# Threshold attention and a GELU MLP: scores of two query slots in one visit, three PSUM banks per head

## The chip, the cores and the metric

The kernel runs on one core of a Trainium2 chip. The metric is the device time of one execution in microseconds; the median of several runs is compared. The engines are named as in the profile: PE (TensorE matmul), PEld (its weight loads), DVE (VectorE), ACT (ScalarE), POOL (GpSimd) and SP (SyncE, which here only issues DMAs).

## The reference

Attention over 8 batches, 8 heads, 576 positions, head dimension 64, with a threshold in place of a plain softmax, and then two matmuls with an exact GELU between them. All is float32.

```
scores = q @ k.T / sqrt(64)
keep   = scores >= max(scores, -1) - tau          # others count as -1e9
attn   = exp(scores - max) of the kept; attn /= sum + 1e-9
x      = (attn @ v), laid out as (8*576, 8*64) = (4608, 512)
out    = gelu(x @ w_in) @ w_out                   # w_in 512x2048, w_out 2048x512
```

## The kernel before

The 64 heads are taken as 32 pairs, two heads of 64 rows on the 128 partitions. Four pairs belong to one batch. The first four pairs ("early") are worked through in another manner while the weights arrive and are converted; the change starts just behind them, and the 28 later pairs are what matters here.

A late pair has five slots: four of 128 queries (i = 0 to 3) and one, i = NC = 4, with the last 64 queries of both heads. For one slot, the kernel issues

1. `scores` (L394): PE forms q times k, 128 queries by 576 keys, for head e = 0 and e = 1. The two heads use the upper and the lower 64 rows of the array at the same time. Each head has a tile `sc` of two PSUM banks with 288 columns in each; there are two such tiles (`bufs=2`), four banks. Slot NC needs one tile only, with all 128 rows.
2. `softmax_head` (L406): for each head a maximum on DVE (L415, `nmx`), a threshold on POOL (L416, `thr`), the exp on ACT (L418), which writes the tile `p` in SBUF.
3. `softmax_tail` (L421): for each head one DVE pass (L434) that compares the scores with the threshold, multiplies the exps by the outcome and sums the row. It is the last reader of `sc`.
4. `turn_p` (L488): DVE transposes `p` in blocks of 32 into `turned_p`. `regroup` (L504) then lets SP issue the DMAs that bring it into `pT`, the layout that the next matmul needs: eight for slots 0 and 1, eight for slots 2 and 3, four for NC.

When a pair is through, `divisors` (L466) turns and spreads the row sums. In the next pair, at slot WEIGH = 2, `weigh_v` (L522) multiplies `pT` by v in two calls of 320 and 256 columns, each into a PSUM tile `xT`, and ACT copies it to `xall` (L547), the input of the MLP. There is one `pT` for each head, so the DMAs of a pair wait until the weighing of the pair before is done. `divide` (L556) multiplies by the divisors on POOL. `scale_q` and `turn_qk` prepare q and k of the next pair on ACT and DVE.

The MLP is issued in small steps between the slots. `block_steps` (L602) is a generator over one block of 256 tokens: a tile `hT` takes eight matmuls (L613) of 256 columns, four for each of two groups of 128 features; `gelus` (L573) puts its GELU on ACT, with up to `lag` tiles left waiting; then `o_ps` (L628) takes 2 x 16 matmuls of 512 columns. `fill` (L637) draws steps as long as a debt of PE time lasts. The debt of a slot comes from a goal for the number of blocks done by that slot (`GOAL`) times a share by slot:

```
    PARTS = 1.3, 1.3, 0.2, 1.3, 0.9
```

GELU and exp use different tables on ACT; `table` (L596) loads the one for exp again, ahead of the next exps, if a GELU ran since. `hT`, `o_ps`, `xT` and a few early tiles share four PSUM banks (tag "mm"), so all eight banks are in use. The order on each engine is the program's order: the kernel is written under a manual schedule.

The last ten blocks of the MLP come after all attention, as a recursive (Strassen-like) product (`last_blocks`, L973); it uses the same two tags of banks.

Of the kernel before, what the change touches and what calls it, by code (L numbers as in the profile page):

```python
# [18 lines left out]
def kernel(  # L19
# [28 lines left out]
    nc = tc.nc  # L48
# [30 lines left out]
    dram = ctx.enter_context(tc.tile_pool(name="dram", bufs=1, space=bass.MemoryType.DRAM))  # L79
    ps = ctx.enter_context(tc.tile_pool(name="ps", bufs=4, space=PSUM))  # L80

# [62 lines left out]
    nc.vector.memset(zeros, 0.0)  # L144
    idle = ps.tile([P, 2 * P], FP32, tag="mm", name="idle")
    for _ in range(3):
# [154 lines left out]
    def turn_qk_early(p):  # L301
# [12 lines left out]
        for name in "qk":  # L314
            t = s[name]
            tr = ps.tile([P, NC, P], FP32, tag="mm", name="tr")
            for c in range(NC):
                for e in range(2):
                    nc.tensor.matmul(tr[e * D:(e + 1) * D, c, :], lhsT=t[:, e, c, :], rhs=ident, start=True, stop=True)
            src = tr.rearrange("p c s -> p (c s)")  # L320
            if name == "q":
                nc.scalar.activation(qT, src, AF.Copy, bias=0.0, scale=q_scale)
            else:
                copy(kT[:, TAIL:S], src)
        tr = ps.tile([P, NC, P], FP32, tag="mm", name="tr")
        for j, name in enumerate("qk"):
# [12 lines left out]
    def turn_p_early(p, i):  # L339
# [11 lines left out]
        for e in range(n):  # L351
            tr = ps.tile([P, NC, P], FP32, tag="mm", name="tr")
            for c in range(NC):
                turn(tr[:, c, :], e * (S + TAIL) + c * P)
            if i < NC:
                nc.scalar.copy(s["pT"][e][:, 0:NC, i * P:(i + 1) * P], tr)  # L356
# [4 lines left out]
        tails = s["pT"][0][:, NC, :]  # L361
        tr = ps.tile([P, NC, P], FP32, tag="mm", name="tr")
        turn(tr[:, 0, :], MAIN if i < NC else S - P)
# [29 lines left out]

    def scores(p, i):  # L394
        s = st[p]
        n = 1 if i == NC else 2
        sc = s["sc", i] = [ps.tile([P, 2, 512], FP32, tag="sc", name="sc", bufs=2) for _ in range(n)]
        for h in range(2):
            for e in range(n):
                rows = slice(0, P) if i == NC else slice(e * D, (e + 1) * D)  # L400
                lhsT = s["q_tail"] if i == NC else s["qT"][rows, i * P:(i + 1) * P]
                at = h * HALF + (TAIL if p < EARLY and e == 0 else 0)
                nc.tensor.matmul(  # L403
                    sc[e][:, h, 0:HALF], lhsT=lhsT, rhs=s["kT"][rows, at:at + HALF], start=True, stop=True)

    def softmax_head(p, i):  # L406
# [6 lines left out]
        for e in range(n):  # L413
            sc = s["sc", i][e][:, :, 0:HALF]
            nc.vector.tensor_reduce(nmx[:, e:e + 1], sc, axis=AXIS.XY, op=ALU.max, negate=True)  # L415
            nc.gpsimd.tensor_scalar(  # L416
                thr[:, e:e + 1], nmx[:, e:e + 1], -1.0, tau_eff, op0=ALU.mult, op1=ALU.subtract)
            nc.scalar.activation(  # L418
                w[:, e * S:(e + 1) * S].rearrange("p (h s) -> p h s", h=2), sc, AF.Exp, bias=nmx[:, e:e + 1], scale=1.0)

    def softmax_tail(p, i):  # L421
# [10 lines left out]
        for e in range(n):  # L432
            row = w[:, e * S:(e + 1) * S].rearrange("p (h s) -> p h s", h=2)
            nc.vector.scalar_tensor_tensor(  # L434
                row, sc[e][:, :, 0:HALF], thr[:, e:e + 1], row, op0=ALU.is_ge, op1=ALU.mult, accum_out=den[e])
        if p < EARLY:
# [8 lines left out]
    def divide_early(p, lo, hi):  # L445
# [3 lines left out]
        b, hp = divmod(p, HP)  # L449
        tr = ps.tile([P, 512], FP32, tag="mm", name="tr")  # L450
        for i in range(lo // P, -(-hi // P)):
# [69 lines left out]

    def weigh_v(p, lo, hi):  # L522


        b, hp = divmod(p, HP)
        s = st[p]
        xT = ps.tile([P, 512], FP32, tag="mm", name="xT")
        for c in range(KR):
            for e in range(2):
                f = slice(e * D, (e + 1) * D)  # L530
                to = xT[f, 0:hi - lo]
                if p < EARLY:
                    rhs = s["pT"][0 if c == NC else e][:, c, lo:hi]
                else:
                    to = to.rearrange("p (g s) -> p g s", s=2 * Q)
                    rhs = by_64(s["pT"][e])[:, lo // (2 * Q):hi // (2 * Q), c, :]
                nc.tensor.matmul(  # L537
                    to, lhsT=s["v"][:, e, c, :], rhs=rhs, start=(c == 0), stop=(c == KR - 1))
        for n, o, at, size in in_blocks(b, lo, hi):
            if n not in x_blk:  # L540
# [61 lines left out]
    def block_steps(n):  # L602
# [3 lines left out]
        for j in range(N_DF):  # L606
            if j % 2 == 0:
                hT = None
            for c in range(N_DM):
                yield NS_IN, (j * P // PIECE + 1) * N_DM  # L610
                if hT is None:
                    hT = ps.tile([P, 2, TOK], FP32, tag="mm", name="hT")
                nc.tensor.matmul(hT[:, j % 2, :], lhsT=w_in_sb[c][:, j * P:(j + 1) * P], rhs=x_blk[n][:, c, :],  # L613
                                 start=(c == 0), stop=(c == N_DM - 1))
            if j % 2:
                late.append((g, j, hT))
                gelus(lag[0])
        x_free.append(x_at.pop(n))
        for m in range(TOK // P):
            for j in range(N_DF):  # L620
# [5 lines left out]
                if j == 0:  # L626
                    o = ps.tile([P, 512], FP32, tag="mm", name="o_ps")
                nc.tensor.matmul(o[:, 0:d_model], lhsT=g[j][:, m * P:(m + 1) * P], rhs=w_out_sb[j],  # L628
                                 start=(j == 0), stop=(j == N_DF - 1))
            o_sb = op.tile([P, d_model], FP32, tag="o_sb", name="o_sb")  # L630
            nc.scalar.copy(o_sb, o[:, 0:d_model])
            row = n * TOK + m * P
            nc.sync.dma_start(out[row:row + P, :], o_sb)

    mlp = {"n": 0, "steps": None, "next": None, "debt": 0.0, "layer": 0}

    def fill(ns, tokens):  # L637

        mlp["debt"] += ns
        while True:  # L640
# [7 lines left out]
            took, need = mlp["next"]  # L648
            if mlp["debt"] <= 0 or need > converted[0]:
                break  # L650
# [153 lines left out]
    def bank(tag, n):  # L804
        if tag == "sc":
            return ps.tile([P, 2, 512], FP32, tag="sc", name="bank", bufs=2)[:, 0, 0:n]
        return ps.tile([P, 512], FP32, tag="mm", name="bank")[:, 0:n]

# [221 lines left out]

    parts = [(range(2), HP), (range(2, SLOTS), HP)] + [(range(SLOTS), 1)] * (NP - HP)
    slots = []
# [19 lines left out]

    PARTS = 1.3, 1.3, 0.2, 1.3, 0.9

# [5 lines left out]
    for n in range(len(slots) + WEIGH + 1):  # L1060
        p, i = slots[n] if n < len(slots) else divmod(n, SLOTS)
        early = p < EARLY
        last = slots[n - 1] if 0 < n <= len(slots) else None
        if p < NP:
            scores(p, i)
            softmax_head(p, i)
            add_low_bits()
# [4 lines left out]
        elif n == len(slots):  # L1072
            early_end.close()
            weights_first()
        gelus(0)
        if n == BATCH:
            gelus_held()
        table()
        for args in due:
            weigh_v(*args)  # L1080
            divide_early(*args)
        due = []
        if p > EARLY and i == WEIGH:
            for lo, hi in (0, WIDE), (WIDE, S):
                weigh_v(p - 1, lo, hi)
            if p == NP:
                divide(p - 1)
        owed += (goal(n) - goal(n - 1)) * BLK_NS * (PARTS[i] if not early and p < NP else 1.0)
        if early:
# [7 lines left out]
        if p < NP:  # L1097
            softmax_tail(p, i)
        if p < NP and not early:
            turn_p(p, i)  # L1100
        if p < NP and not early:
            if i == 2:
                regroup(p, 1)
            if i > 2:
                regroup(p, i)
            if i == NC:
                divisors(p)
# [10 lines left out]
        if n == BATCH:  # L1118
            for t in pd_tail + [turned_p[:, e, h, :, :] for e in range(2) for h in range(2)]:
                nc.gpsimd.memset(t[:, NB:4 * KR, :], 0.0)  # L1120
        if EARLY < p < NP and i == DIVIDE:
            divide(p - 1)
        if p >= HP and i == 1 and p + 2 < NP:
            loads = load_steps(p + 2)
        if p >= HP:
            next(loads, None)
        if p >= HP and i == 1 and p + 1 < NP or p == HP - 1 and i == 2:
            scale_q(p + 1)
        if p >= HP - 1 and i == 2 and p + 1 < NP:
            turn_qk(p + 1)  # L1130
        convert(0 if n == 0 else 1200 if n < 3 else 2200 if n < BATCH - 1 else 1e9)
        if not early:
            lag[0] = 2 if p < NP else 0
            if n != BATCH:
                fill(owed, tokens)
                owed = 0.0
# [7 lines left out]
        elif n == BATCH + 1:  # L1144
            tokens = S
        elif p > EARLY and i == DIVIDE and p % HP == 0 or p == NP and i == WEIGH:
            tokens = p // HP * S
            leaving += [n for n in AWAY if n in x_blk and (n + 1) * TOK <= tokens]
        elif leaving and i < 2:
            put_away(leaving.pop(0))  # L1150
    fill(1e12, B * S)
    late_end.close()
    last_blocks()

# [31 lines left out]
```

## Time and profile before

| what | value |
|---|---|
| median of 3 runs | 1352.92 us (1352.58 to 1353.92) |
| the profiled execution, its own time | 1353.51 us |
| its span, first to last instruction | 1351.4 us |
| late pairs, from the first weighing in their manner to the 27th | 184.7 to 848.1 us |
| end of the last weighing | 882.6 us |
| granted clock of TensorE | 0.993 over the span, 1.00 in the late pairs |

In the profile, a line as "L418 ACT ACTIVATE p<-sc,nmx" is a group of instructions of one source line, with the tile written before the arrow and those read behind it. Busy time is the time in which an engine had an instruction under way; a matmul's end is modelled, so consecutive matmuls overlap in the records and the distance between their starts is what they cost PE. A float32 matmul is two records. "128*128", "64*128" and "128*64" name the part of the array that a matmul uses, rows by columns. In the timeline, the first number is the start, the second the length of a run of equal instructions, and what stands in brackets is idle time of the engine before it and who ended it.

### The profile page before, as it was taken

How to read it: one execution, taken by the hardware profiler on the slowest of the kernel's cores; microseconds unless marked ns; L12 is line 12 of the kernel's file. 1: busy time of each engine (PE TensorE's matmuls, PEld its weight loads, DVE VectorE, ACT ScalarE, POOL GpSimd, SP SyncE). 2: the span in 40 equal slices, each digit the busy share in tenths (PEclk: the TensorE clock that was granted, in tenths of full speed). 3: DMA queues.
4: the chain of work that ended last, by engine and by line, in shares of the span. 5: the costliest groups of instructions: out<-in, count | busy, mean ns of one | idle time of the engine just before them, and what ended most of it. 6: DMA issues, size and time to landing. Idle time of an engine off the chain costs nothing.

```text
span 1351.4 us, 19821 instructions
## 1 busy us (share of the span) xinstructions
PE 1323.0 (98%) x6282; PEld 893.8 (66%) x6282; DVE 1048.1 (78%) x1997; ACT 605.0 (45%) x1027; POOL 659.0 (49%) x1097
## 2 busy tenths in 40 slices
PE   8799899999999999999999999999999999999998
PEld 6476557467467557557557557568787787877877
DVE  6987677788888888888888888874758698385765
ACT  7876527548547538537638636413201112211120
POOL 5785354555555554554554551144363513635530
PEclk9899999999999999999999999999999999999999
DMA  8642276677777787687687777500000041000003
GB/s 268 187 151 52 58 164 156 146 162 185 155 180 182 161 193 178 160 207 172 153 208 180 155 179 152 117 9 0 1 0 1 14 112 32 0 1 0 1 0 78
DMA packets 209781, 152.39 MB, mean 113 GB/s; under 512 B 113360, under 2 KB 193088, under 8 KB 209680
## 3 DMA queue, kind: packets, MB, share of 16 engines
q1 hardware_dynamic: 188224, 112.53, 37.5%
q0 software_dynamic: 21024, 38.32, 9.9%
q8 instruction: 51, 0.84, 0.3%
q14 instruction: 50, 0.41, 0.1%
q10 hardware_dynamic: 432, 0.30, 0.1%
HBM read 55.97 MB, written 12.52 MB: 51 GB/s over the span
## 4 chain that ended last, share of the span: by engine, by line
PE 93%; DVE 3%; ACT 3%; DMA 1%; issue 1%; SPq 0%; POOL 0%; DVEq 0%; ACTq 0%; POOLq 0%
PE bank L801 34%; PE o_ps L628 17%; PE hT L613 16%; PE sc L403 14%; PE xT L537 11%; ACT p L418 1%; DMA x<-xall 1%; DVE nmx L415 1%; DVE p L434 1%; PE tr L349 1%; ACT pT L356 1%; DVE power L212 0%; ACT power L202 0%; DVE power L210 0%; PE tr L456 0%
## 5 line engine op out<-in xcount | busy, mean ns | idle before, releaser
L418 ACT ACTIVATE p<-sc,nmx 128x576 f32<-128x576 f32 x288 | 201.9, 738 | 284.0 <-DVE nmx L415 283.7
L434 DVE SCALAR_TENSOR_TENSOR p<-sc,thr,p 128x576 f32<-128x576 f32 x288 | 225.3, 816 | 70.1 <-ACT p L418 68.6
L416 POOL TENSOR_SCALAR thr<-nmx,tau_eff 128x1 f32<-128x1 f32 x288 | 88.0, 307 | 368.0 <-DVE nmx L415 355.8
L415 DVE TENSOR_REDUCE nmx<-sc 128x1 f32<-128x576 f32 x288 | 205.4, 750 | 53.5 <-PE sc L403 52.3
L613 PE MATMUL hT<-xall,w_in 128*128 128x256 f32 x1024 | 241.8, 385 | 0.0
L628 PE MATMUL o_ps<-w_out,g 128*128 128x512 f32 x512 | 236.8, 603 | 0.0
L613 PEld LDWEIGHTS hT<-xall,w_in 128*128 128x128 f32 x1024 | 189.4, 190 | 50.0 <-issue 23.0
L683 DVE TENSOR_TENSOR c<-c,bank 128x320 f32<-128x320 f32 x304 | 147.3, 488 | 33.6 <-PE bank L801 20.1
L683 DVE TENSOR_TENSOR o<-o,bank 128x256 f32<-128x256 f32 x240 | 99.8, 420 | 93.7 <-PE bank L801 88.7
L403 PE MATMUL sc<-kT,qT 64*128 64x288 f32 x960 | 161.8, 431 | 9.3 <-DVE p L434 8.6
L537 PE MATMUL xT<-pT,v 128*64 128x256 f32 (+1 forms) x1280 | 169.3, 418 | 0.8 <-DVE pT L360 0.5
L628 PEld LDWEIGHTS o_ps<-w_out,g 128*128 128x128 f32 x512 | 93.1, 190 | 109.1 <-issue 106.8
L498 DVE STREAM_TRANSPOSE turned_p<-p 128x1152 f32<-128x1152 f32 x112 | 154.4, 1378 | 3.9
L403 PEld LDWEIGHTS sc<-kT,qT 64*128 64x128 f32 x960 | 92.4, 187 | 83.8 <-issue 69.7
L537 PEld LDWEIGHTS xT<-pT,v 128*64 128x64 f32 x1280 | 93.0, 140 | 75.4 <-issue 15.1
L801 PE MATMUL bank<-w_out,c 128*128 128x256 f32 x480 | 120.2, 381 | 0.5 <-DVE o L683 0.5
L269 POOL DMA_DIRECT2D v<-in_v_dram x208 | 110.9, 536 | 3.9 <-issue 1.9
L801 PEld LDWEIGHTS bank<-w_out,c 128*128 128x128 f32 x480 | 89.9, 190 | 18.8 <-DVE o L683 3.0
L854 ACT ACTIVATE c<-c 128x320 f32<-128x320 f32 (+1 forms) x80 | 46.9, 623 | 114.6 <-DVE c L683 114.6
L683 POOL TENSOR_TENSOR c<-c,g 128x320 f32<-128x320 f32 (+1 forms) x40 | 50.5, 1271 | 67.4 <-DVE c L683 67.4
L801 PE MATMUL bank<-t_out,c 128*128 128x256 f32 x320 | 82.7, 381 | 0.0
L801 PE MATMUL bank<-t_out,g 128*128 128x256 f32 x320 | 82.1, 379 | 0.0
(179 smaller groups left out, 1775.1 us busy)
## 6 DMA issues: line engine op xcount, KB each, us to landing
pT<-turned_p SPq DMA_DIRECT2D x448, 160.0 KB, 3.6
pT<-pd_tail SPq DMA_DIRECT2D x112, 80.0 KB, 3.0
q<-in_q_dram POOLq DMA_DIRECT2D x104, 72.0 KB, 3.4
k<-in_k_dram POOLq DMA_DIRECT2D x104, 72.0 KB, 3.2
inv<-turned SPq DMA_DIRECT2D x54, 128.0 KB, 3.9
v<-in_v_dram POOLq DMA_DIRECT2D x156, 40.0 KB, 3.1
out_dram<-o SPq DMA_DIRECT2D x40, 128.0 KB, 2.4
xall<-in_moe_w_out_dram POOLq DMA_DIRECT2D x9, 512.0 KB, 3.8
```

Source lines behind the costliest of these rows:

```text
L269: eng.dma_start(t[r:P:4, e, 0:n, :], rows[:, r * KR:r * KR + n, :])
L403: nc.tensor.matmul(sc[e][:, h, 0:HALF], lhsT=lhsT, rhs=s["kT"][rows, at:at + HALF], start=True, stop=True)
L415: nc.vector.tensor_reduce(nmx[:, e:e + 1], sc, axis=AXIS.XY, op=ALU.max, negate=True)
L416: nc.gpsimd.tensor_scalar(thr[:, e:e + 1], nmx[:, e:e + 1], -1.0, tau_eff, op0=ALU.mult, op1=ALU.subtract)
L418: nc.scalar.activation(w[:, e * S:(e + 1) * S].rearrange("p (h s) -> p h s", h=2), sc, AF.Exp, bias=nmx[:, e:e + 1], scale=1.0)
L434: nc.vector.scalar_tensor_tensor(row, sc[e][:, :, 0:HALF], thr[:, e:e + 1], row, op0=ALU.is_ge, op1=ALU.mult, accum_out=den[e])
L498: nc.vector.transpose(turned_p[:, :, i // 2, 0:NB, i % 2 * Q:(i % 2 + 1) * Q], w.rearrange("p (e b i) -> p e b i", e=2, i=Q))
L537: nc.tensor.matmul(to, lhsT=s["v"][:, e, c, :], rhs=rhs, start=(c == 0), stop=(c == KR - 1))
L613: nc.tensor.matmul(hT[:, j % 2, :], lhsT=w_in_sb[c][:, j * P:(j + 1) * P], rhs=x_blk[n][:, c, :], start=(c == 0), stop=(c == N_DM - 1))
L628: nc.tensor.matmul(o[:, 0:d_model], lhsT=g[j][:, m * P:(m + 1) * P], rhs=w_out_sb[j], start=(j == 0), stop=(j == N_DF - 1))
L683: eng.tensor_tensor(out, a, b, op=ALU.add)
L801: nc.tensor.matmul(to, lhsT=l, rhs=r, start=start and k == 0, stop=k == len(pairs) - 1, skip_group_check=not start)
```

## The change

From slot n = JOIN = BATCH + 2 = 22 on, the third slot of the first late pair:

- The scores of slots 0 and 1, and those of 2 and 3, are formed in one visit of PE ("joint"): 12 matmuls of 192 columns in place of twice four of 288. A head's tile has now three banks; slot i takes columns 0 to 191 of each, slot i+1 columns 192 to 383. Two such tiles take six banks; the tag "mm" keeps two. The pools are closed and opened anew at JOIN, and once more before `last_blocks` (four and 2 x 2 banks again).
- The slots of a pair come in the order 0, 1, NC, 2, 3. `pos` is the place in a pair. The heads and tails of the softmax of both slots are issued one after the other: four maxima and exps, then four masked passes, then a transpose (the second one in the next place).
- `weigh_v` takes both spans in one call, and its two outputs lie in one tile of the tag "sc" in place of two tiles of "mm". The copies to `xall` come after all its matmuls.
- `regroup` of slots 0, 1 and of NC comes at place 2, that of slots 2 and 3 at place 4, right before `divisors`. `divide`, the loads of q, k and v, `scale_q` and `turn_qk` keep their places, which now belong to other slots.
- GELUs are issued right behind their tile (`lag` 0 in place of 2), and once layer one is under way `fill` goes on until the open `hT` tile is complete (`close`). The shares by place are 1.1, 1.1, 0.6, 1.1, 1.1.

```diff
-    ps = ctx.enter_context(tc.tile_pool(name="ps", bufs=4, space=PSUM))
+    def lay_out_banks(name, mm, width):
+        banks.close()
+        space["pool"] = banks.enter_context(tc.tile_pool(name=name, bufs=mm, space=PSUM, reuse_waits="tile"))
+        space["width"] = width
+    def score_banks(name):
+        return space["pool"].tile([P, space["width"], 512], FP32, tag="sc", name=name, bufs=2)
+    lay_out_banks("ps", 4, 2)
...
-    def scores(p, i):
+    def scores(p, i, both=False):
...
+        units = [i, i + 1] if both else [i]
+        wide = S // 3 if both else HALF
+        sc = [score_banks("sc") for _ in range(n)]
+        for k, c in enumerate(units):
+            s["sc", c] = [t[:, 0:S // wide, k * wide:(k + 1) * wide] for t in sc]
+            for h in range(S // wide):
+                for e in range(n):
...
+                    nc.tensor.matmul(
+                        s["sc", c][e][:, h, :], lhsT=lhsT, rhs=s["kT"][rows, at:at + wide], start=True, stop=True)
...
-    def fill(ns, tokens):
+    def fill(ns, tokens, close=False):
...
-            if mlp["debt"] <= 0 or need > converted[0]:
+            if not (close and mlp["open"]) and mlp["debt"] <= 0 or need > converted[0]:
                 break
...
-    parts = [(range(2), HP), (range(2, SLOTS), HP)] + [(range(SLOTS), 1)] * (NP - HP)
+    parts = [(range(2), HP), (range(2, SLOTS), HP)] + [((0, 1, NC, 2, 3), 1)] * (NP - HP)
...
-    PARTS = 1.3, 1.3, 0.2, 1.3, 0.9
+    PARTS = 1.1, 1.1, 0.6, 1.1, 1.1
+    JOIN = BATCH + 2
...
+        pos = n % SLOTS
+        if n == JOIN:
+            gelus(0)
+            lay_out_banks("ps_joined", 2, 3)
+        single = n < JOIN or i == NC
+        if n > JOIN and (single or i % 2 == 0):
+            table()
         if p < NP:
-            scores(p, i)
-            softmax_head(p, i)
+            if single:
+                scores(p, i)
+                softmax_head(p, i)
+            elif i % 2 == 0:
+                scores(p, i, both=True)
+                softmax_head(p, i)
+                softmax_head(p, i + 1)
...
-        if p > EARLY and i == WEIGH:
-            for lo, hi in (0, WIDE), (WIDE, S):
-                weigh_v(p - 1, lo, hi)
+        if p > EARLY and pos == WEIGH:
+            xT = score_banks("xT")
+            weigh_v(p - 1, [(0, WIDE), (WIDE, S)], [xT[:, half, :] for half in range(2)])
...
-            softmax_tail(p, i)
+            if single:
+                softmax_tail(p, i)
+            elif i % 2 == 0:
+                softmax_tail(p, i)
+                softmax_tail(p, i + 1)
         if p < NP and not early:
             turn_p(p, i)
-        if p < NP and not early:
-            if i == 2:
+            if pos == 2:
                 regroup(p, 1)
-            if i > 2:
-                regroup(p, i)
-            if i == NC:
+                regroup(p, NC)
+            if pos == 4:
+                regroup(p, 3)
                 divisors(p)
...
-            lag[0] = 2 if p < NP else 0
+            lag[0] = 2 if n < JOIN - 1 else 0
             if n != BATCH:
-                fill(owed, tokens)
+                fill(owed, tokens, n == JOIN - 1 or n >= JOIN and mlp["layer"] == 1)
...
     late_end.close()
+    lay_out_banks("ps_last", 4, 2)
     last_blocks()
```

## The prediction

> **What bounds the kernel now.** I read the busy shares first, then the table by stretches for the 26 pairs of heads between the first and the 27th weighing after the early part (184.7 to 848.1 us), then the timeline of one pair.
>
> ```profile
> PE 1323.0 (98%) x6282; PEld 893.8 (66%) x6282; DVE 1048.1 (78%) x1997; ACT 605.0 (45%) x1027; POOL 659.0 (49%) x1097
> ```
> ```profile
> 184.70:848.10 663.40, 661.66 (x3252) 403.22 (x3250) 566.31 (x1014) 380.44 (x579) 346.24 (x709) 1.00 0.75 171
> ```
>
> The columns of the second are the stretch, PE, PEld, DVE, ACT and POOL busy, clock, DMA share, GB/s. A pair takes 663.4/26 = 25.52 us; PE is busy in nearly all of it, DVE for 566.3/26 = 21.8. PE bounds the stage, DVE stands 3.7 us behind.
>
> ```profile
> 523.63 0.70 PE L613 MATMUL hT<-xall,w_in 128*128 128x256 f32 x2
> 524.26 1.24 PE L403 MATMUL sc<-kT,qT 64*128 64x288 f32 x8
> 525.43 3.72 PE L613 MATMUL hT<-xall,w_in 128*128 128x256 f32 x16
> 525.60 1.42 DVE L415 TENSOR_REDUCE nmx<-sc 128x1 f32<-128x576 f32 x2
> 526.39 1.41 ACT L418 ACTIVATE p<-sc,nmx 128x576 f32<-128x576 f32 x2 [0.77 <-DVE nmx L415]
> 527.24 0.82 DVE L434 SCALAR_TENSOR_TENSOR p<-sc,thr,p 128x576 f32<-128x576 f32 x1 [0.21 <-ACT p L418]
> ...
> 527.98 0.81 DVE L434 SCALAR_TENSOR_TENSOR p<-sc,thr,p 128x576 f32<-128x576 f32 x1
> ...
> 528.83 1.38 DVE L498 STREAM_TRANSPOSE turned_p<-p 128x1152 f32<-128x1152 f32 x1
> ...
> 529.96 2.32 PE L613 MATMUL hT<-xall,w_in 128*128 128x256 f32 x10
> ...
> 531.79 0.82 DVE L434 SCALAR_TENSOR_TENSOR p<-sc,thr,p 128x576 f32<-128x576 f32 x1 [0.88 <-ACT p L418]
> ...
> 532.21 1.76 PE L403 MATMUL sc<-kT,qT 64*128 64x288 f32 x8
> ```
>
> Starts are what to read on PE. A matmul in float32 is two records; those of hT start 0.216 apart (10 from 529.96, then scores at 532.21: 2.16 plus 0.09). The two records at 523.63 should give way after 0.43 but the scores start 0.63 later, and the scores need 1.17 for 4 x 0.242 = 0.97: **each change between the full array (128*128) and a divided one (64*128, 128*64) costs PE 0.20 us**. The visit at 532.21 shows the other loss: it had to wait for the DVE pass of 531.79 to free its second bank, and ran 1.76 in place of 1.24. Such waits, read from starts over all visits, sum to some 8 us in the stage.
>
> **The Trainium skill.** "TensorEngine Tiling (Array Packing)", Key Properties, says that a change of tiling mode drains the engine; the trace agrees and prices it (0.20). "TensorE: Matmul & The Clock Gate", LDWEIGHTS (loading the stationary operand), gives columns/1.2 ns, 107 ns for 128 columns, so an estimate of 0.163 for a record of 192 columns (its stream, 0.160, the longer of the two) stands. "PSUM — Partial Sum Buffer", PSUM bank collisions raise a hardware error, says that engines may not use one bank at once. No run here shows an error, but the changed program's waits follow it, and this decides the case below.
>
> **The change, part by part.** *Switches.* Counted in the order of PE's instructions in the two programs after the early part, 245 mode changes become 161: 84 x 0.198 = **-16.6 us**. *Narrower matmuls:* 24 records x 0.163 in place of 16 x 0.242 (two side by side): 1.95 for 1.94 a joint visit, +0.4 in all. *Waits of before* that fall: **-8**. *Gelus:* 55 pairs of table loads become 38 (1.28 us each on ACT); ACT is 57% busy in the stage and bounds nothing, so nothing on the path.
>
> *The new chain.* Both slots of a visit lie in the same three banks of a head. In the changed program the reduce of slot 1 waits for the exp of slot 0 on the same tile, the first masked pass waits for the exp of slot 1, and the first reduce waits for the last of the visit's 12 matmuls. Counting from the first reduce, with the trace's times (reduce 0.75, next 0.68 later; exp 0.74, next 0.67; masked pass 0.74 apart, 0.82 long; 0.035 from DVE to ACT, 0.10 from ACT to DVE): reduces of slot 0 at 0 and 0.68; exps 0.78 and 1.46; reduces of slot 1 at 1.62 and 2.30; exps 2.41 and 3.09; masked passes 3.25, 3.99, 4.73, 5.47; transposes 6.33 and 7.63; DVE free at 8.93. PE sees the first head's banks (A) free at 5.68, the second's (B) at 6.42. The first reduce comes 2.25 after the visit starts (10 starts of 0.163, 0.27 for the first, 0.32 for the last, 0.03). So **a joint visit holds A for 7.93 us and B for 8.67**; PE's own work in it is 2.15, and the layer work behind it must cover the rest, 5.8 or 6.5 us.
>
> What stands behind is fixed in the program: 16 hT matmuls (7.0 us with the change of mode), 7 of layer two (6.1), or, where a tile was closed early, 8 hT (3.6), 4 to 6 of layer two (3.5 to 5.3). And DVE comes late to the second visit of a pair: after visit (2,3) it needs 8.93 + 0.55 (divisors), after which visit (0,1) starts up to 0.81 late. Stepping the 26 pairs through (each visit starts when PE is through and its banks are free, each reduce 2.25 later or when DVE is free), PE waits
> - before visit (0,1), for B: four times 2.9 (8 hT or 4 of layer two behind visit (2,3)), once 1.2, ten times 0.3 (7 of layer two): 15.8;
> - before slot 4 (NC), for A: three times 2.5 and once 2.2 (8 hT or 4), four times 1.3, once 0.7, six times 0.5: 18.5;
> - before visit (2,3), in the five pairs where no layer work follows the weighing, for ACT's four copies of xT, which now hold B: 1.1 each, 5.5.
>
> Together **+39.8 us**. At the JOIN slot the banks are laid out anew: NC waits for the last copy of o (0.9), visit (2,3) comes straight behind it and waits for its masked pass (2.7), visit (0,1) has 3 of layer two for cover (3.8): **+7.3**.
>
> Behind each waiting score matmul stands all of PE's later work, the layer matmuls too: nothing fills the gap.
>
> *Two mm banks in place of four:* a first hT tile behind a visit ends at 5.7, its gelu (exps end at 6.1, load 1.28, gelu 0.60) at 8.0; the third tile, which takes its bank, starts after 11: nothing. *turn_qk* moves behind NC: DVE there needs 4.9 from reduce to last transpose and is free before visit (2,3)'s first reduce in every pair: nothing.
>
> *Transfers moved.* The eight regroupings of slots 2 and 3 now follow the second transpose of visit (2,3), 9.0 after its first reduce. SP issues eight in 7 x 0.66 and one lands in 3.6: done at 17.3. The weighing starts there at about 16.3 with half of them; its second half, which needs all, at 19. They are covered by 1.7 us. Regrouping of slots 0, 1 and NC starts when the weighing frees pT, as before. POOL's thresholds (0.3) come before its loads in each visit and are ready 2 us ahead of the masked pass.
>
> *Sum:* -16.6 + 0.4 - 8 + 39.8 + 7.3 = +22.9. The profiled execution took 1353.51 for a span of 1351.4; its time is 0.6 over the median of the runs, 1352.92, so 1376.4 for a profiled execution and **1376** for the median. A check of the step-through: with no waits it gives 645 us for the 26 pairs against 663.4, the 18 us of switches and old waits; with them 679.3.
>
> Bounds of the chain, which no row of before shows: 0.2 us shorter for each visit gives 672 for the stage in place of 679, 0.2 longer 686, half a microsecond longer (exps behind a gelu's table load) 697.
>
> **Rivals.** *The cover suffices (faster).* If the first reduce could start on slot 0 while PE writes slot 1, 1.3 after the visit's start, and the exps ran beside the reduces, A would be free at 6.5, B at 7.2, DVE at 9.7: the stage steps to 654, the JOIN costs 4.5, and the kernel takes 1352.9 - 9.4 + 4.5 = **1348**. It decides from a hold of A of about 6.7 on. PE's surplus of switches speaks for it; the waits of the changed program, bank by bank, against it. *Transfers as well (slower still).* The 1.7 us of cover are gone when a landing takes 5.3 in place of 3.6; the pairs would then wait for pT instead of a bank, and a further 0.7 us in each gives **1393**. The DMA share of 0.75 speaks for it, that no weighing of before waits for DMA against. *ACT late*, 0.5 us in each visit's chain: 697 for the stage, **1393** too. *It does nothing*: PE's waits just match the switches, 1353; that needs the junction waits at 17 in place of 39.8.
>
> **Numbers.** Forecast (1376, own range 1362 to 1387) 0.78; later still 0.12; faster rival 0.07; no change 0.03. The range of 1359 to 1392 leaves out the faster rival and the far end of the later ones. About 0.2% is what a measurement here can tell from no change. Faster 0.07, same 0.03, slower 0.90.
>
> **What would show it.** Right: PE's wait for scores on DVE's masked pass rises from 1.6 us in the stage to tens; the group of reduces gets ACT's exp as releaser; DVE's first reduce 2.2 us after a visit; mode changes down by a third; table loads 38. The stage would last some 679 us. Wrong: PE without waits there (the faster rival), waits of xT on pT's transfers, or a gap before exps that a table load fills.

## The result and the profile after

The changed kernel takes 1404.88 us (median of 4 runs, 1396.01 to 1406.24), the kernel before 1353.42 in the same comparison: a ratio of 1.037 [1.032, 1.041]. The forecast was 1376 with a range of 1359 to 1392. The direction was right; the loss is 51 us in place of 23, and the time lies above the range.

First the page of the kernel after, the engines' busy time; then the table by stretches from the first to the 27th weighing (stretch, PE, PEld, DVE, ACT and POOL busy, clock, DMA share, GB/s).

```profile
PE 1332.0 (95%) x6722; PEld 942.2 (67%) x6722; DVE 1031.0 (74%) x1997; ACT 563.1 (40%) x976; POOL 660.9 (47%) x1097
```
```profile
187.40:897.00 709.60, 670.57 (x3665) 450.73 (x3664) 549.60 (x1014) 340.95 (x532) 346.15 (x709) 0.98 0.76 160
```

The span is 1402.0 us. The first weighing starts 2.7 later than before, the 26 pairs behind it take 709.6 in place of 663.4, the last weighing ends at 932.0 in place of 882.6, and what follows takes 470.0 in place of 468.8. So 46 of the 51 us lie in the 26 pairs. PE now stands idle for 39.0 us of them (709.60 - 670.57; before 663.40 - 661.66 = 1.7), and the mean clock there is 0.98.

PE's waits over the whole span (us in total, times, longest):

```profile
PE sc L422 <- DVE p L455: 38.9, 29, 3.3
PE sc L422 <- ACT xall L566: 15.4, 8, 6.9
...
PE xT L556 <- DMA pT<-turned_p: 1.4, 4, 0.6
```

The first line is the wait that was forecast, for the masked pass that frees a score bank. Over the whole span it was 15.8 us before, but 14 to 17 us of either sum lie outside the 26 pairs. In the pairs alone it is 21.6 us over 19 places, and in the kernel before:

```profile
PE sc L403 <- DVE p L434: 1.6, 2, 1.3
```

The second line, for ACT's copy of xT, holds three long waits that were not forecast. The timeline shows the first kind at work, in a pair with two hT tiles behind the visit:

```profile
408.37 2.22 PE L422 MATMUL sc<-kT,qT 64*128 64x192 f32 x24
...
410.62 2.99 DVE L437 TENSOR_REDUCE nmx<-sc 128x1 f32<-128x576 f32 x4 [4.66 <-PE sc L422]
...
415.30 0.81 DVE L455 SCALAR_TENSOR_TENSOR p<-sc,thr,p 128x576 f32<-128x576 f32 x1
...
416.27 0.56 PE L422 MATMUL sc<-kT,qT 64*128 64x192 f32 x2 [2.03 <-DVE p L455]
```

The first reduce comes 2.25 after the visit's start; the third masked pass, the last reader of the first head's banks, starts at 415.30; the next visit starts 7.90 after this one. Forecast: 2.25 and 7.93. Over the joint visits the third masked pass ends 5.50 after the first reduce and the fourth 6.23 (medians). In the prediction's chain they start at 4.73 and 5.47 and last 0.82, so they end at 5.55 and 6.29; its 5.68 and 6.42 are when PE learns of it, 0.13 later. The third reduce starts 0.90 after the second where 0.67 is usual, so it does wait for the first head's exp, but too briefly to show as the releaser of its group.

The second kind, in a pair in which a block of x is put away:

```profile
514.37 0.59 SPq L689 DMA_DIRECT2D x<-xall  x1
...
515.08 0.59 PE L422 MATMUL sc<-kT,qT 64*128 64x192 f32 x2
...
518.13 0.55 ACT L566 COPY xall<-xT 128x64 f32<-128x64 f32 x3 [5.36 <-DMA x<-xall]
...
518.74 3.17 PE L422 MATMUL sc<-kT,qT 64*128 64x192 f32 x22 [3.06 <-ACT xall L566]
```

`put_away` (L689) writes a block of `xall` to DRAM, and the next copies of xT go into its place. ACT stands idle for 5.36 us until the write is through. xT now lies in the second head's score banks, so PE gets through the first head's first records at 515.08 and then stands until the copies are done. This happens at 518.7, 631.1 and 739.5, for 3.2, 7.1 and 3.4 us by the starts, 13.7 in all.

The third loss is the clock. The table by stretches, with edges on the clock's own steps of 3.41 us (first group of columns as above):

```profile
512.93:516.34 3.41, 2.74 (x13) 1.91 (x11) 1.01 (x4) 0.00 (x0) 0.20 (x1) 1.00 0.73 185
516.34:519.76 3.42, 1.02 (x12) 1.02 (x14) 0.00 (x0) 1.61 (x4) 0.00 (x0) 1.00 0.98 291
519.76:523.17 3.41, 3.41 (x17) 2.79 (x14) 1.70 (x3) 3.36 (x6) 0.58 (x2) 0.51 0.89 199
523.17:526.58 3.41, 3.41 (x17) 2.94 (x17) 3.20 (x7) 3.22 (x5) 2.46 (x6) 0.99 0.88 150
```

PE was busy for 1.02 of 3.42 us, and in the next 3.41 us it ran at half clock. There are eight such stretches in the 26 pairs, six of 3.41 and two of 6.83 us. At half speed they cost at most 17.1 us, an estimate: half of their length, though PE also stood idle for 3.3 us inside the two long ones. The kernel before has none in these pairs. The four runs differ here: the fastest, 1396.01, had a mean granted clock of 0.985 over its span, the others 0.979 to 0.980. Only one of these others was traced, so which stretches the fastest was spared isn't known.

### The profile page after: what moved, and what is told of

The parts are those of the page before. It is cut to its first block, busy times and chain, and to the rows that moved or that the text cites. A ratio compares the mean times of both kernels' runs of the same rounds, so it can differ in the third digit from the quotient of the medians.

```text
span 1402.0 us, 20418 instructions
## 1 busy us (share of the span) xinstructions
PE 1332.0 (95%) x6722; PEld 942.2 (67%) x6722; DVE 1031.0 (74%) x1997; ACT 563.1 (40%) x976; POOL 660.9 (47%) x1097
## 4 chain that ended last, share of the span: by engine, by line
PE 71%; DVE 9%; DMA 8%; SPq 7%; ACT 3%; issue 2%; DVEq 0%; POOL 0%; ACTq 0%; POOLq 0%
PE bank L824 32%; PE hT L633 10%; PE xT L556 9%; PE o_ps L650 9%; PE sc L422 9%; SPq L541 4%; DMA pT<-turned_p 4%; DVE p L455 3%; DMA turned<-turned 3%; DVE turned_p L519 2%; DVE nmx L437 2%; ACT p L440 2%; DMA pT<-pd_tail 1%; DMA x<-xall 1%; SPq L507 1%
## 5 line engine op out<-in xcount | busy, mean ns | idle before, releaser
L455 DVE SCALAR_TENSOR_TENSOR p<-sc,thr,p 128x576 f32<-128x576 f32 x288 | 220.9, 815 | 45.3 <-ACT p L440 44.2
L633 PE MATMUL hT<-xall,w_in 128*128 128x256 f32 x1024 | 234.0, 384 | 0.0
L650 PE MATMUL o_ps<-w_out,g 128*128 128x512 f32 x512 | 233.6, 604 | 0.0
L633 PEld LDWEIGHTS hT<-xall,w_in 128*128 128x128 f32 x1024 | 192.4, 191 | 38.8 <-issue 13.0
L422 PE MATMUL sc<-kT,qT 64*128 64x192 f32 (+1 forms) x1400 | 162.1, 359 | 36.3 <-DVE p L455 20.9
L422 PEld LDWEIGHTS sc<-kT,qT 64*128 64x128 f32 x1400 | 132.8, 200 | 75.3 <-issue 54.2
L556 PE MATMUL xT<-pT,v 128*64 128x256 f32 (+1 forms) x1280 | 173.9, 421 | 2.4 <-DMA pT<-turned_p 1.4
L556 PEld LDWEIGHTS xT<-pT,v 128*64 128x64 f32 x1280 | 99.2, 141 | 75.2 <-issue 25.4
L519 DVE STREAM_TRANSPOSE turned_p<-p 128x1152 f32<-128x1152 f32 x112 | 147.6, 1355 | 0.1
```

Of the source, the lines that this page charges most:

```text
L422: nc.tensor.matmul(s["sc", c][e][:, h, :], lhsT=lhsT, rhs=s["kT"][rows, at:at + wide], start=True, stop=True)
L455: nc.vector.scalar_tensor_tensor(row, sc[e], thr[:, e:e + 1], row, op0=ALU.is_ge, op1=ALU.mult, accum_out=den[e])
L519: nc.vector.transpose(turned_p[:, :, i // 2, 0:NB, i % 2 * Q:(i % 2 + 1) * Q], w.rearrange("p (e b i) -> p e b i", e=2, i=Q))
L556: nc.tensor.matmul(to, lhsT=s["v"][:, e, c, :], rhs=rhs, start=(c == 0), stop=(c == KR - 1))
```

## The experiments

Three causes were put up after the result. **R**: PE waits for the release of score banks, as forecast. **P**: it waits for the put-away write through ACT's copies. **C**: long waits halve the clock behind them, and so cost more than their length. A fourth question is which part of the change brings R: the joint visits, or layer one in whole tiles. "The stage" is the 26 pairs; before it is 663.4 us, after 709.6.

### The put-away write from another queue

```diff
-        nc.sync.dma_start(away[n], x_blk.pop(n))
+        nc.gpsimd.dma_start(away[n], x_blk.pop(n))
```

> One edit to the changed kernel: the write that puts an input block of the last stage away (x<-xall, five times 512 KB) is issued by POOL in place of SP. Theory P: in the changed kernel SP reaches this write late, behind the loads of inv, ACT's copies of xT wait for it to land, and since xT now lies in the score banks PE waits too, 3.2 + 7.1 + 3.4 = 13.7 us in three pairs, with a stretch of half clock behind each. Then these waits go, and the time falls by 14 to 20 us, to 1384 to 1391. Rival (the wait moves): the copies find another late transfer, and less than 5 us are gained, 1400 or more.

Measured 1388.63 us, 1.027 [1.025, 1.029] of before: 16 less than the changed kernel. Stage 692.0. PE's waits:

```profile
PE sc L422 <- DVE p L455: 39.4, 30, 3.3
PE xT L556 <- DMA pT<-turned_p: 7.0, 7, 2.2
...
PE sc L422 <- ACT xall L566: 2.2, 5, 0.4
```

The wait for ACT fell from 15.4 to 2.2, that for DVE stayed (in the stage 21.6, as in the changed kernel), and the half clock cost at most 6.8 us in place of 17.1. P is shown, with the clock as its companion. A new wait came up, for the transfers into pT. What is left of the stage exceeds the forecast 679.3 by 12.7 us, about what these transfers (7.0) and the half clock (6.8) come to.

### PE kept busy ahead of visit (0,1) and of NC

To the kernel just shown, matmuls on weights whose output nobody reads are added, until PE has 6.5 us of work behind the last visit.

```diff
+        if JOIN < n < len(slots) and pos in (0, 2):
+            keep_busy()
```

> The kernel with the write on POOL, and in addition, wherever a joint visit has a closed hT tile and less than 6.5 us of layer work behind it, PE is given matmuls of 256 columns on weights whose product nobody reads, up to that cover. They fill waits that PE has anyway: stepped through, the stage grows by 2.4 us and the waits of over 2 us fall from eight to two. Theory C: PE's clock is halved for 3.4 us behind each window in which it stood idle for more than half, about 1.5 us a time, so the extra work makes the kernel faster by 5 to 9 us against the write on POOL alone. Rival: the stretches of half clock have another cause (load, time), they stay, and the kernel is 2 to 3 us slower than without the extra matmuls.

Measured 1385.82, 1.024 [1.023, 1.026]: 2.8 less, though PE has more to do. No stretch of half clock is left in the stage, where four were. So it is the idle time of PE that brings the half clock, as C has it; but the gain is under the 5 to 9 us that were expected. The half clock had fallen to 6.8 us with the put-away, and the added matmuls took some of that back.

### Readers ordered by head

In a joint visit of the changed kernel, the maxima and masked passes go first head of both slots, then second head.

```diff
-        for e in range(n):
+        for e, i in [(e, i) for e in range(n) for i in slots_in]:
```

> One edit to the changed kernel: in a joint visit the reduces, exps and masked passes go by head (both slots of head 0, then both of head 1) in place of by slot. The work is the same; the chain on a head's three banks becomes two reduces, two exps, two masked passes. Theory R (release of the banks): banks A come free 4.66 us after the first reduce in place of 5.68, B 6.14 in place of 6.42, DVE 8.65 in place of 8.93; stepped through, the stage takes 666.0 in place of 679.3 us and the waits of over 2 us fall from eight to four, so 13 us less and some 5 us of half clock less: 1384 to 1392. Rival: PE's waits do not hang on this order (two mm banks, gelus behind their tile), and the time stays within 4 us of 1404.

Measured 1395.56, 1.031 [1.029, 1.034]: 9 less by the medians, with single runs of 1390 to 1399 against 1396 to 1406, so the size is uncertain. Stage 699.2; PE's wait for DVE in the stage falls from 21.6 to 13.0. The last masked pass on the first head's banks ends 4.55 after the first reduce in place of 5.50. R is right in kind, and its gain was smaller than expected; the wait for pT rises from 1.4 to 5.1, the waits for ACT (14.2) stay, with three stretches of half clock behind the long ones.

### Layer one not closed to whole tiles

```diff
-                fill(owed, tokens, n == JOIN - 1 or n >= JOIN and mlp["layer"] == 1)
+                fill(owed, tokens, n == JOIN - 1)
```

> One edit to the changed kernel: fill no longer goes on to the end of an open hT tile (the one time at the change of banks apart), so layer one is cut anywhere and the work behind the visits is even, 5.6 to 6.2 us each. Theory R: stepped through, the stage takes 664.3 in place of 679.3, the waits lie between 0.2 and 1.2 us and none is over 2, so no half clock except behind the put-away blocks: 1404 less 15 less 8 to 10, 1379 to 1384. Rival: an hT tile left open over a visit holds one of only two mm banks and delays gelus, and the time stays or rises, 1400 or more.

Measured 1393.53, 1.030 [1.029, 1.032]: 11 less, between the theory's range and the rival's. The wait for DVE in the stage falls from 21.6 to 3.7, so most of it did hang on the closing. Another takes its place (whole span):

```profile
PE sc L422 <- DVE p L455: 21.5, 17, 3.3
PE sc L422 <- ACT xall L566: 13.3, 3, 5.7
PE hT L633 <- ACT g L605: 10.8, 9, 2.3
...
PE o_ps L650 <- ACT g L605: 2.3, 1, 2.3
```

A tile left open over a visit is closed behind it, its GELU stands behind the visit's four exps, and with two mm banks the tile after next waits for it. At 312.77 us of this run PE has waited 1.24 us for a GELU that started at 312.12, behind the four exps and a table load of 1.28.

### The put-away and the order by head together, then open tiles too, then other shares

These build on one another: the first joins the first and the third edit, the second adds the fourth, the last changes the shares.

> The changed kernel with two edits at once: the put-away write from POOL, and the maxima, exps and masked passes of a joint visit ordered by head (bank A's readers first). Whole tiles of layer one are kept. Theory (waits for the release of the score banks plus the put-away wait plus the half clock): with the write away from SP and A free earlier, the step model of the prediction gives 666 us for the 26 pairs, the pT waits of the run with the put-away on POOL add about 5, and no stretch of half clock should be left but one or two: stage 668 to 674, time 1364 to 1372. Rival, the two gains simply add (-16 and -9): 1378 to 1381. Rival, the gain is lost to a new wait: above 1384.

Measured 1381.63, 1.023 [1.020, 1.026], stage 688.5: near the rival, where the gains simply add. The wait for pT is 10.6 us over 11 places, not 5:

```profile
PE sc L422 <- DVE p L467: 29.6, 24, 3.3
PE xT L568 <- DMA pT<-turned_p: 10.6, 11, 2.7
```

With the wait for ACT at 2.2 and 3.4 of half clock, that makes 16 of the 22 us by which the stage exceeds the step model's 666 (the prediction's way of stepping the pairs through, with the new order); the other 6 were not located.

> As e5_head_away, and the fill is no longer closed to whole tiles. Theory: the step model gives 647 us for the 26 pairs, the waits of layer one for GELUs (two mm banks, a tile left open over a visit) add about 13, the pT waits about 5: stage 662 to 668, time 1357 to 1364. Rival, gains simply add (-16, -9, -11): 1367 to 1370. Rival, open tiles undo all of it: 1375 or more.

Measured 1384.51, 1.024 [1.022, 1.026]: no gain from open tiles here, the second rival. The waits for score banks are gone from the stage (0.3 us); PE waits 16.2 + 2.8 for GELUs and 9.0 for pT in their place.

> As e6_three with shares PARTS of 1.1, 1.1, 0.4, 1.2, 1.2 in place of 1.1, 1.1, 0.6, 1.1, 1.1, so that more layer work lies between the visits that wait for bank A. Step model 640.5 us for the 26 pairs, with 18 of the other waits 656 to 661: time 1350 to 1357, level with the kernel before. Rival, the GELU and pT waits grow by what is moved: 1360 or more.

```diff
-    PARTS = 1.1, 1.1, 0.6, 1.1, 1.1
+    PARTS = 1.1, 1.1, 0.4, 1.2, 1.2
```

Measured 1375.28, 1.017 [1.016, 1.019], the fastest with joint visits, and 9 less than with the old shares. The time is in the rival's range, but not for its reason: the GELU waits fell from 19.0 to 16.8 and the pT waits stayed (9.1). No wait for a score bank is left in the stage, which takes 678.6 us, some 20 more than expected; beyond these waits and 5.1 of half clock the excess was not located.

### One part alone in the kernel before

Both whole tiles and GELUs right behind their tile:

```diff
-            lag[0] = 2 if p < NP else 0
+            lag[0] = 2 if n < BATCH + 1 else 0
...
-                fill(owed, tokens)
+                fill(owed, tokens, n == BATCH + 1 or n >= BATCH + 2 and mlp["layer"] == 1)
```

> The kernel before with one part of the change alone, from the third slot of the first late pair on: GELUs right behind their tile (lag 0) and layer one closed to whole tiles; scores slot by slot, four mm banks, old order of slots. Theory, the loss is that of the joint visits, and this part by itself is nearly free with slots of two score banks per head: 1350 to 1357. Rival, whole tiles by themselves shorten the cover of some slots and cost a good part of the 51 us: 1362 or more.

Measured 1385.52, 1.025 [1.023, 1.026], so 33 us slower with no joint visit at all: the rival. The two halves apart, first the `lag` line alone:

> The kernel before with GELUs right behind their tile (lag 0) from the third slot of the first late pair on, nothing closed to whole tiles. Theory: the cover of each slot stays as it is (the numbers of layer matmuls between visits are those of before), GELU and exp table loads stay hidden: 1350 to 1357. Rival: GELUs ahead of the exps delay the chain of each slot and cost half or more of the 33 us that both parts cost together: 1368 or more.

Measured 1353.85, 1.001 [1.000, 1.002]. Then the `fill` line alone:

> The kernel before with layer one closed to whole tiles, GELUs two tiles late as before. Theory: all of the 33 us of both parts together comes from the rounding, which leaves some slots with no layer work ahead of them (five gaps with none in the program, the time between such visits goes up by 2.3 to 3.3 us, and a stretch of half clock follows in some): 1381 to 1388, three to five stretches of half clock. Rival, the GELUs share in it: 1355 to 1372.

Measured 1382.26 (1373.08 to 1383.05), 1.020 [1.016, 1.023]: the rounding to tiles is nearly the whole of it. Stage 686.4, so 23 us lie there; the first weighing starts 6.4 later than in the kernel before. The timeline of this kernel, at a slot that the rounding left without layer work:

```profile
414.29 1.13 PE L403 MATMUL sc<-kT,q_tail 128*128 128x288 f32 x4
...
415.36 0.75 PE L403 MATMUL sc<-kT,qT 64*128 64x288 f32 x2
...
417.10 0.82 DVE L434 SCALAR_TENSOR_TENSOR p<-sc,thr,p 128x576 f32<-128x576 f32 x1 [0.88 <-ACT p L418]
...
418.07 1.21 PE L403 MATMUL sc<-kT,qT 64*128 64x288 f32 x6 [1.97 <-DVE p L434]
```

The next visit follows NC directly and stops for NC's masked pass. Half clock follows: four stretches in this kernel's stage, at most 8.5 us.

### The changed kernel without its joint visits

```diff
-        single = n < JOIN or i == NC
+        single = True
```

> The changed kernel with all slots in visits of their own (288-wide score matmuls, two of the three banks of a tile used); order of slots 0, 1, NC, 2, 3, two mm banks, xT in a score tile, whole tiles and the shares are kept. Theory: the parts other than the joint visits bring most of the loss themselves: put-away wait about 14, four to six gaps without layer work about 12, half clock about 12, one mode change more for each pair 5: 1385 to 1402. Rival: the joint visits are what costs, and without them only put-away wait and mode changes are left: 1366 to 1374.

Measured 1435.97, 1.061 [1.059, 1.063]: 31 us slower than the changed kernel, and beyond the theory's range. All waits for ACT's copies together were 4.9 us rather than 14, so this term of the theory was wrong too. xT lies in a score tile there as well, so how long PE waits for the write also depends on how the slots fall in time. Most of the excess is in the visits: read from starts, what visits of scores take beyond their median length (half clock included) sums to 53 us, against 35 in the changed kernel and 7 before. Half clock costs at most 20.5. In this company **the joint visits themselves are a gain**.

### The put-away write in the kernel before

The first edit, made to the kernel before.

> The kernel before with the put-away write issued by POOL in place of SP, nothing else. Theory: in the kernel before ACT's xT copies wait for this write too (14.4 us in all), but xT lies in mm banks that nobody needs soon, so the place of the write does not matter: same time within 0.3%, 1349 to 1356. Rival: the put-away costs the kernel before something as well, and the 16 us gained by the same edit of the changed kernel are not the price of the moved xT: 1346 or less.

Measured 1350.69 (18 runs) against 1352.73 (29 runs), 0.998 [0.997, 0.999]: within the theory's range, though its reason is not quite right, since the place of the write does matter by 2 us. The same edit gained 16 us in the changed kernel, so nearly all of that price came with the change. This is the one version that is faster than both kernels. The timeline of the kernel before shows where:

```profile
600.33 0.43 ACT L547 COPY xall<-xT 128x128 f32<-128x128 f32 x2 [4.00 <-DMA x<-xall]
...
602.90 0.27 ACT L547 COPY xall<-xT 128x128 f32<-128x128 f32 x1 [2.14 <-DMA x<-xall]
603.06 1.38 ACT L418 ACTIVATE p<-sc,nmx 128x576 f32<-128x576 f32 x2
...
604.88 1.21 PE L403 MATMUL sc<-kT,q_tail 128*128 128x288 f32 x4 [1.31 <-DVE p L434]
```

The exps stand behind the copies on ACT; they are late, so is the masked pass, and PE waits 1.31. With the write on POOL this pair takes 24.91 in place of 27.11 us; another, four pairs on, takes 26.96 in place of 25.93, and why was not looked into.

## Why the prediction was right in direction and wrong in size

**Switches, table loads, narrower matmuls: as forecast.** The group of GELU table loads has 38 in place of 55:

```profile
L605 ACT ACT_TABLE_LOAD x38 | 48.8, 1283 | 0.7
```

From the first to the 27th weighing PE changes mode 151 times in place of 230, in the order of its instructions. An undisturbed joint visit takes 2.15 us, as forecast, and its records start 0.163 apart. The weight loads, which it put at 107 ns, have records of 187 ns here (median), but these overlap and did not lengthen the visit.

**The chain and the waits for banks: as forecast.** The 7.93 us that a joint visit holds the first head's banks measured 7.90. The step-through behind the 679.3, taken pair by pair, met the first five pairs within 0.2 us: 28.10, 27.12, 27.17, 27.52, 25.57, measured 28.11, 26.95, 27.17, 27.46, 25.50. (Only the sum, 679.3, stands in the prediction; its values for single pairs, here and below, were given after the result.) Read from starts, the waits for banks come to some 30 us in place of 34.3: before visit (0,1) four of 2.8 and one of 1.1, before NC four of 2.2 and four of 1.1, the others 0.5 or less. The prediction's check with no waits, 645 us, does not fit its terms: 663.4 less 16.6 and 8 is 639, plus 0.4. The difference is about the 5.5 for the copies of xT; it does not enter the forecast.

**The step that failed: no wait for the copies of xT outside "the five pairs where no layer work follows the weighing".** For those five the prediction was right. Their visit (2,3) stops after two records until ACT has copied, and takes 3.17 us in place of 2.15, five times 1.02 against five times 1.1:

```profile
302.05 0.59 PE L422 MATMUL sc<-kT,qT 64*128 64x192 f32 x2
302.19 0.83 ACT L566 COPY xall<-xT 128x128 f32<-128x128 f32 x4 [3.27 <-PE xT L556]
303.07 2.21 PE L422 MATMUL sc<-kT,qT 64*128 64x192 f32 x22 [0.43 <-ACT xall L566]
```

For all other pairs the prediction has no such wait, and gives no reason. In three of these the copies waited for the put-away write, and PE for them, 13.7 us. By the measure just used, the length of the visit beyond 2.15, the three visits lost 4.6, 9.5 and 5.9 us, half clock inside them included. The step-through had 27.26, 25.53, 26.02 us for these pairs, measured were 32.69, 35.61, 33.55. That is 23.0 of the 30.3 us by which the stage exceeds the 679.3: 13.7 of waits and at most 8.5 of half clock. The experiment bears it out: with the write on POOL these three pairs together take 14.9 less, and the kernel 16. The trace of before had the wait in plain sight ("ACT xall L547 <- DMA x<-xall: 14.4, 4, 5.1"). It was passed over, since PE did not wait there on its account; in the changed kernel, with xT in the score banks, it came onto PE's path, and even before it cost 2 us by way of the exps.

**No term for the clock.** The second step that failed: the sum held every wait at its own length. Eight stretches of half clock added at most 17.1 us, 8.5 of them in five pairs other than those three; the other 23 pairs together exceeded their forecast by 7.3. "TensorE: Matmul & The Clock Gate", Part 1: The HAM clock gate, of the Trainium skill names a free-running window of 3413 ns and a fall to half rate after an idle window. The trace agrees on the length of the window and on the half, but the window need not be idle: one with PE busy for 1.02 us, or 1.54 in the kernel closed to whole tiles, sufficed.

**JOIN, +7.3:** the waits there were 0.84, 2.29 and 2.92, together 6.05, and two stretches of half clock follow them (at 164.9 and 175.1 us). That the first weighing still starts only 2.7 later was not explained.

**"Two mm banks: nothing"** held in the changed kernel only because its tiles are closed: with open tiles PE waits 13 us for GELUs. **The transfers, "covered by 1.7 us"**, held while the other waits gave them time (1.4 us of waiting); without the put-away wait they cost 7.0 to 10.6. So the rival "transfers as well" is what comes next, not what happened.

**What the sum did not separate.** The cover behind each visit was counted in whole tiles, as the program has it, so the 39.8 us of junction waits held the price of the rounding without naming it. The runs name it: closing costs the kernel before 29.5 us alone, GELUs right behind their tile 1. The joint visits gain 31 us where all else is kept, more than their switches alone. The new order of the slots and the new shares were not taken back by themselves. How the parts share the loss beyond this isn't additive, and stays open.

## What to carry to other kernels

When a buffer is moved, follow each of its readers back through everything that can make it late, in the trace of before too: a wait that hurts nobody there hurts as soon as the buffer is one that the bound engine needs. Work that covers a fixed latency must not be rounded to units as large as that latency; here tiles of 3.5 us left some visits with none. Price an idle gap of PE of about 2 us or more at more than its length: in these traces half clock followed when PE stood idle for more than 1.9 us of a step of 3.41.

## What was not expected of the hardware

Whether a wait halves the clock depends on where it falls on the 3.41 us steps. In the changed kernel, a wait of 2.03 us before 416.27 left PE busy for 1.21 of its step, and the next ran at half clock; one as long (both visits start 2.41 after the record before them; the second at 445.38) was split over two steps, and the clock stayed:

```profile
413.98:417.40 3.42, 1.21 (x8) 0.72 (x8) 3.42 (x9) 3.37 (x4) 3.42 (x8) 1.00 0.78 128
417.40:420.81 3.41, 3.41 (x23) 2.97 (x19) 3.07 (x6) 0.40 (x2) 2.38 (x5) 0.51 0.36 80
...
441.29:444.70 3.41, 2.06 (x10) 1.48 (x8) 3.19 (x7) 3.23 (x4) 2.42 (x7) 1.00 0.82 130
444.70:448.12 3.42, 2.56 (x24) 2.21 (x24) 3.42 (x6) 2.18 (x4) 3.42 (x8) 1.00 0.22 47
448.12:451.53 3.41, 3.41 (x17) 2.93 (x16) 3.20 (x8) 1.62 (x3) 1.45 (x5) 1.00 0.65 124
```

In this kernel's pairs, steps at full clock with PE busy for 1.4 us or less were followed by half clock, those with 1.95 and more were not. All kept traces together, from 200 to 1300 us, narrow the bound without fixing it: every step at full clock with PE busy for less than 1.5 us was followed by half clock. Between 1.5 and 1.9 both occur, 1.82 followed in the kernel with whole tiles and `lag` 0, 1.52 not in the last with other shares. Above 1.9 a single one was, of 2.22 us in the kernel with single visits. Busy time rests on modelled ends of matmuls, so the edge may be sharper than it looks.
